# Handing out two relus and one operand split ahead of the values' product, and one weight split behind a bank's copy

## The chip, the core and the metric

One core of a Trainium2 chip runs the kernel. Its engines work from queues of their own, each in order: TensorE (PE in the profile; PEld are its weight loads), VectorE (DVE), ScalarE (ACT), GpSimd (POOL) and SyncE (SP), which issues most transfers. An instruction waits for the results of other engines at the head of its queue, and everything behind it in that queue waits with it. The metric is the device time of one execution in microseconds, as the median of several runs.

## What is computed

```
xn = layernorm(x)                                  # x: 2048 x 512, fp32
q, k, v = split(xn @ wqkv)                         # 32 heads of 16
phi(t) = where(t > 0, t + 1, exp(t)) + 1e-6
kv = sum_s phi(k)_s v_s^T ;  z = sum_s phi(k)_s     # for each head
att = (phi(q) kv) / (phi(q) z + 1e-6) @ wo
mlp = relu(xn @ w1 + b1)^2 @ w2 + b2                # 512 -> 1376 -> 512
out = x + att + mlp
```

## The kernel before

**Precision.** A factor of a product is split into an upper half (a copy rounded to the matmul's format, made on ScalarE) and a lower half (the rest, a subtraction on VectorE). `three` and `product` then run three matmuls for each pair: upper by upper, upper by lower, lower by upper. `split(h, l, src, eh, el)` makes both halves. So each operand costs one ScalarE and one VectorE instruction before the third matmul can run; the first two need the upper half of the weights only.

**Two parts.** The first part (to about 100 us) normalises x, transposes it, projects the keys, and sums `kx`, the keys by the tokens. The second part is the loop over n = 0 and 1, each for two blocks of 512 tokens, x1 and x2. There, chunks of wq and w1 (256 columns at a time) are multiplied with both blocks by Winograd's scheme: seven half-size products (`A11`, `A12`, `S1` to `S4`, `A22`) in place of eight. Their factors are sums of quarters of the weights (S1 to S4) and of the tokens (T1 to T4), each split in two halves. The loop over p goes over the chunks: q, w1, q, and then w1 to the end.

**Places.** For the products there are four banks, `banks`, taken as A, `before`, B and C. At p = 0, TensorE runs product A (`A11`), product B (`A12`) and product C (`S1` with T1), six matmuls each; then `matrix(0)` and `matrix(1)`, three each, into `pm0` and `pm1`; then the second product into A (`S2` with T2), `matrix(2)`, the second into C (`S4`), `matrix(3)`, and `S3` with T3. The banks of `pz` and `pz0b` are among those that `banks` takes over, C's being that of `pz`. Operand halves stand in `aop`; the raw chunks of weights and S1 to S4 share six places, "raw".

**Around the change.** The last chunk of w1 has only 96 columns and is computed by itself for both blocks: `pz` (x1) and `pz0b` (x2), with `plain_1`. Between them run the last matmuls of `kx`. `values()` (line 870) multiplies `kx` by wv into `pkv` (lines 871 to 878), masks it by heads into `kv` on VectorE (line 880), and splits that into `kvt` (upper half on ScalarE, lower on VectorE). `matrix(j)` multiplies `kvt` by wo; its results are the attention's 512 x 512 matrix.

**The order by hand.** The program is in a manual schedule: each engine runs its instructions in the order of the text. `extra` is a list of small pieces of work (splits, differences for T, operands), and `more()` takes the next few off it, by a table of counts. `do(list, k)` takes k pieces. When `values()` is called in the old text, five pieces are left: the lower half of T1's second part; the split of S1 and S2; the lower half of T2's second part; the split of `A22`; the split of S3 and S4. The call of `more()` behind `values()` takes the first two of these, and `do(extra, len(extra))` the last three, behind the two relus (line 476, a helper's; called at 953 and 954), which move `pz` and `pz0b` out of their banks into `r2c`.

**w2.** `piece_2(f, at)` loads chunk f of w2 (256 KB) and returns two pieces, the upper half on ScalarE and the lower on VectorE. For the last chunk (f = 10, 96 rows in three loads), the upper half's piece also has five casts on GpSimd, which lay out a quarter of it four times (`w2q`), and the lower half is two subtractions. `next_2(t)` (line 974) does what is left of the present chunk, and calls `piece_2` for the next, so that its load is issued. `next_2(0)`, at line 986, does the last chunk's halves and issues the load of chunk 0. Inside p, `c11` (line 1050) is product A copied out of its bank on ScalarE; VectorE adds it to B (line 1055). The first matmuls that read the last chunk of w2 are those of `last_2` at p = 1.

The order of instructions by engine around the change, in the old text:

```
ScalarE: A's operand | kvt upper | S1,S2 upper | relu pz | relu pz0b | A22 upper | S3,S4 upper | w2 upper | c11 | t5 | T3 ...
VectorE: A's operand | kv | kvt lower | T1 lower | S1,S2 lower | T2 lower | A22 lower | S3,S4 lower | w2 lower x2 | q <- B + c11 | T3 lower x2 ...
```

Of the kernel before, what the change touches and what calls it, by code (L numbers as in the profile page):

```python
# [18 lines left out]
def kernel(  # L19
# [58 lines left out]
    def bank(name, tag="ps"):  # L78
        return psum.tile([P, 512], F32, name=name, tag=tag)

    def w512(name, tag, bufs):
        return work.tile([P, 512], F32, name=name, tag=tag, bufs=bufs)
# [26 lines left out]
    def copy(eng, o, i, bias=0.0):  # L109
        if eng == "act":  # L110
            nc.scalar.activation(o, i, AF.Copy, bias=bias)  # L111
        elif bias:
            ENG[eng].tensor_scalar(o, i, bias, None, op0=OP.add)
        else:
            ENG[eng].tensor_copy(o, i)

    def split(h, l, src, eh, el):
        copy(eh, h, src)
        ENG[el].tensor_tensor(out=l, in0=src, in1=f32(h), op=OP.subtract)  # L119
# [76 lines left out]
    def piece_2(f, at):  # L196

        h, l = w2s[f] = [w2r[at // 2][:, at % 2 * 2 + u] for u in range(2)]
        if f < NF - 1:
            t = raw(f"r2_{f}", w2[f * P:(f + 1) * P, :])  # L200
            return [lambda: copy("act", h, t), lambda: rest_of(l, t, h)]


        t = w512(f"r2_{f}", "raw", 6)
        for a, o, n in units(f):
            nc.sync.dma_start(t[a:a + n], w2[o:o + n, :])

        def high():
            copy("act", h, t)
            copy("pool", l[2 * Q:], h[:2 * Q])  # L210
            if "q" not in w2s:
                w2s["q"] = work.tile([P, D], F32R, name="w2q", tag="w2q")
                for k in range(TB):
                    copy("pool", w2s["q"][k * Q:(k + 1) * Q], h[2 * Q:3 * Q])

        def low():
            rest_of(l[:2 * Q], t[:2 * Q], h[:2 * Q])
            rest_of(h[3 * Q:], t[3 * Q:], h[3 * Q:])

        return [high, low]  # L220
# [191 lines left out]
    def steps_of(t, j, done=False, parts=False):  # L412


        o = q[t][:, j]
        tiles = []
        blocks = lambda ap: ap.rearrange("p (r c) -> p r c", c=32)
        heads_of = lambda ap: ap.rearrange("p (h d) -> p h d", h=H)
        by_heads = lambda ap: ap.rearrange("p (r h) d -> p r h d", h=2)

        def weighted():
            pz = w512(f"pz{t}_{j}", "p", 6)
            tiles.append(pz)
            nc.scalar.activation(pz, o, AF.Identity, bias=zc[:, 1, j:j + 1], scale=zc[:, 0, j:j + 1])

        def sums():
            pt = w512(f"pt{t}_{j}", "p", 6)
            den = small.tile([P, H], F32, name=f"dt{t}_{j}", tag="den")
            nc.vector.transpose(blocks(pt), blocks(tiles[0]))
            nc.vector.tensor_reduce(den, heads_of(pt), axis=AX.X, op=OP.add)  # L430
            tiles.append(den)

        def quotients():
            pz, den = tiles
            nc.vector.tensor_scalar(den, den, 1e-6, None, op0=OP.add)
            nc.vector.reciprocal(den, den)
            nc.vector.transpose(by_heads(heads_of(pz)), by_heads(den[:, :, None].to_broadcast([P, H, D // H])))

        def divide():
            nc.vector.scalar_tensor_tensor(o, o, 1e-6, tiles[0], op0=OP.add, op1=OP.mult)  # L440

        def into_parts():
            a = aT[t, j] = places.pop(0)
            split(a[:, 0], a[:, 1], o, "act", "dve")

        return [lambda: phi_T(o, o)][done:] + [weighted, sums, quotients, divide] + [into_parts][:parts]
# [28 lines left out]
    def relu(o, i, f):  # L475
        nc.scalar.activation(o, i, AF.Relu, bias=b1s[:, f:f + 1])

    def plain_1(ps, w, x):

        for j in range(NJ):  # L480
            three(ps, [w[:, u, j * P:(j + 1) * P] for u in range(2)],
                  [x[u][:, j, :] for u in range(2)], j == 0, j == NJ - 1)

    def product(ps, a, b, first=False, last=False):

        for j in range(2):
            for n, (u, v) in enumerate(PASSES):
                nc.tensor.matmul(ps, lhsT=a[u][:, j * P:(j + 1) * P], rhs=b[v][:, j, :],  # L488
                                 start=first and j == 0 and n == 0, stop=last and j == 1 and n == 2,
                                 skip_group_check=True)  # L490
# [50 lines left out]
    for i0 in range(0, NT, TB):  # L541
# [5 lines left out]
        n = TB if i0 >= NPE else NPE - NDVE  # L547
# [175 lines left out]
    def do(what, k=1):  # L723
        for _ in range(k):
            if what:
                what.pop(0)()
# [39 lines left out]
    extra, counts = [], [[0, 0, 0, 0, 0, 1, 1, 0, 0, 1, 2, 2, 0, 1, 4, 1, 2]]  # L766

    def more(i=None):

        if i is None or i > 12:  # L770
            do(extra, counts[0].pop(0))
# [98 lines left out]
    def values():  # L870
        ps = bank("pkv", "acc")
        for c in range(NJ):
            for j in range(NJ):
                at = slice(j * P, (j + 1) * P)

                nc.tensor.matmul(ps[:, at], lhsT=wvs[:, c, at], rhs=kxs[c // 2][:, c % 2, at],  # L876
                                 start=c == 0 and j == 0, stop=c == NJ - 1 and j == NJ - 1,
                                 skip_group_check=True)
        t = w512("kv", "p", 6)
        nc.vector.tensor_tensor(out=t.rearrange("p (j d) -> p j d", j=NJ), in0=ps.rearrange("p (j d) -> p j d", j=NJ),  # L880
                                in1=heads[:, None, :].to_broadcast([P, NJ, P]), op=OP.mult)
        kvt[0] = work.tile([P, 2, 512], F32R, name="kvt", tag="r3")
        split(kvt[0][:, 0], kvt[0][:, 1], t, "act", "dve")
# [16 lines left out]
    for n in range(2):  # L900
# [42 lines left out]
        if n == 0:  # L943

            more()
            pz2 = bank("pz0b")
            plain_1(pz2, z, x2)
            more()
            values()
            more()  # L950

            rz = r2[1]
            relu(rz, pz, NF - 1)
            relu(r2[NF - 1], pz2, NF - 1)
            do(extra, len(extra))
            w2next = piece_2(NF - 1, 0)
        else:
            w2next = []
            pz = bank(f"pz{n}", "acc")
            plain_1(pz, z, x1)  # L960
# [13 lines left out]
        def next_2(t):  # L974

            do(w2next, 2 - highs.pop(0))
            if t + 1 < NF and (n == 0 or t >= TB - 1):
                f = w2order[t + 1]
                w2next.extend(piece_2(f, place(f)))

        def high_2():
            do(w2next)
            highs[0] = 1

        highs = [0] * NF
        next_2(0)


        banks = [bank(f"b{n}_{k}") for k in range(4)]
# [29 lines left out]
        def step(k=1):  # L1019

            for _ in range(k):
                do(steps[t1] or steps[t2])

        for p in range(NO + 1):
# [24 lines left out]
            if kind:  # L1049
                c11 = w512(f"c11_{n}_{p}", "p", 6)  # L1050
                copy("act", c11, A)
                product(B, A12, [x[:, 2:] for x in x1], True, True)
                if kind == "w":
                    high_2()
                nc.vector.tensor_tensor(out=c11 if kind == "w" else q[t1][:, fa], in0=B, in1=c11, op=OP.add)
                if kind == "w":
                    relu(c11, c11, fa)
                else:
                    steps[t1] += steps_of(t1, fa, parts=True)
                step(at_p[0])  # L1060
# [261 lines left out]
```

## Time and profile before

| | us |
|---|---|
| median of 3 runs | 415.05 (414.95 to 415.22) |
| the profiled execution | 415.3 |
| its span in the trace | 413.6 |
| TensorE busy, of the span | 408.6 |
| mean granted clock of TensorE | 0.998 |

A row of the timeline reads: start, length, engine, line and operation, output and inputs by the program's names, shape, count, and in brackets the idle time of the engine just before it with the instruction that ended it. Rows with a count are several instructions of one kind in a row, merged. The chain of waits is followed back from the last instruction to what released it, and its pieces are listed in order of time. Matmuls are pipelined and their ends are modelled, so a wait shows in the weight loads (PEld) more plainly than in the matmuls. A row of the windows reads: the stretch, its length, then for TensorE, weight loads, VectorE, ScalarE and GpSimd the busy time and in brackets the count, then the granted clock, the share of the transfer engines and their rate in GB/s.

### The profile page before, as it was taken

How to read it: one execution, taken by the hardware profiler on the slowest of the kernel's cores; microseconds unless marked ns; L12 is line 12 of the kernel's file. 1: busy time of each engine (PE TensorE's matmuls, PEld its weight loads, DVE VectorE, ACT ScalarE, POOL GpSimd, SP SyncE). 2: the span in 40 equal slices, each digit the busy share in tenths (PEclk: the TensorE clock that was granted, in tenths of full speed). 3: DMA queues.
4: the chain of work that ended last, by engine and by line, in shares of the span. 5: the costliest groups of instructions: out<-in, count | busy, mean ns of one | idle time of the engine just before them, and what ended most of it. 6: DMA issues, size and time to landing. Idle time of an engine off the chain costs nothing.

```text
span 413.6 us, 5427 instructions
## 1 busy us (share of the span) xinstructions
PE 408.6 (99%) x1835; PEld 336.9 (81%) x1835; DVE 314.5 (76%) x584; ACT 270.2 (65%) x487; POOL 50.0 (12%) x70
## 2 busy tenths in 40 slices
PE   8999999999999999999999999999999999999996
PEld 7788888888888888888878888888888888878885
DVE  6895667797699898998439996468989685449843
ACT  5867767756668888789547731567588857737420
POOL 3241222230130000020000040100000200000310
PEclk9999999999999999999999999999999999999999
DMA  7789572710321312264267991411120871025602
GB/s 248 272 247 353 204 228 101 234 48 2 102 77 52 101 41 72 93 177 78 89 246 251 385 198 75 129 52 48 54 79 25 228 183 47 2 86 168 103 0 101
DMA packets 44925, 54.62 MB, mean 132 GB/s; under 512 B 7905, under 2 KB 29153, under 8 KB 43618
## 3 DMA queue, kind: packets, MB, share of 16 engines
q1 hardware_dynamic: 42594, 50.09, 37.1%
q0 software_dynamic: 2304, 4.20, 6.5%
q8 instruction: 14, 0.23, 0.2%
q14 instruction: 13, 0.11, 0.1%
HBM read 41.16 MB, written 13.11 MB: 131 GB/s over the span
## 4 chain that ended last, share of the span: by engine, by line
PE 97%; DMA 1%; ACT 0%; SPq 0%; DVE 0%; issue 0%
PE acc L130 37%; PE b L488 32%; PE kx L389 11%; PE pk L370 11%; PE acc L499 2%; PE pz L130 1%; DMA rk<-in_A_wqkv_dram 1%; PE pkv L876 1%; PE pm L130 1%; PE pz0b L130 1%; PE b L130 1%; PE pt L309 1%; PE acc L506 0%; SPq L159 0%; PE end L130 0%; ACT wkh L111 0%
## 5 line engine op out<-in xcount | busy, mean ns | idle before, releaser
L130 PE MATMUL acc<-w2r,s 128*128 128x512 f32 x477 | 112.9, 390 | 0.0
L130 PEld LDWEIGHTS acc<-w2r,s 128*128 128x128 f32 x477 | 89.4, 188 | 19.3 <-issue 0.7
L488 PE MATMUL b<-T,aop 128*128 128x512 f32 x336 | 83.9, 390 | 0.0
L488 PEld LDWEIGHTS b<-T,aop 128*128 128x128 f32 x336 | 62.8, 188 | 13.9 <-DVE aop L119 0.4
L389 PE MATMUL kx<-pk,tok 128*128 128x512 f32 x192 | 46.8, 392 | 0.0
L389 PEld LDWEIGHTS kx<-pk,tok 128*128 128x128 f32 x192 | 35.6, 188 | 8.0 <-DVE pk L378 0.6
L488 PE MATMUL b<-xs0h,aop 128*128 128x512 f32 x112 | 36.9, 390 | 0.0
L1005 POOL DMA_DIRECT2D res<-in_B_b_dram x16 | 14.1, 1099 | 182.4 <-DVE dt L430 64.1
L130 PE MATMUL acc<-mh,aTsr 128*128 128x512 f32 x112 | 35.6, 389 | 0.0
L119 POOL TENSOR_TENSOR tok<-xp,tok 128x512 fp32r<-128x512 f32 x16 | 22.3, 1393 | 55.1 <-ACT tok L111 55.1
L1013 DVE TENSOR_TENSOR res<-acc,res 128x512 f32<-128x512 f32 x16 | 11.0, 692 | 23.1 <-PE acc L130 18.5
L122 DVE TENSOR_TENSOR w2r<-r,w2r 128x512 fp32r<-128x512 f32 (+2 forms) x35 | 25.2, 721 | 0.1
L111 ACT ACTIVATE aop<-S 128x512 fp32r<-128x512 f32 x28 | 17.5, 624 | 11.1 <-DVE S L705 11.1
L130 PEld LDWEIGHTS acc<-mh,aTsr 128*128 128x128 f32 x112 | 21.0, 188 | 4.4
L488 PEld LDWEIGHTS b<-xs0h,aop 128*128 128x128 f32 x112 | 21.0, 188 | 4.3
L119 DVE TENSOR_TENSOR aop<-S,aop 128x512 fp32r<-128x512 f32 x28 | 19.5, 697 | 4.3 <-ACT aop L111 3.9
L119 DVE TENSOR_TENSOR s<-c,s 128x512 fp32r<-128x512 f32 x20 | 13.6, 689 | 11.0 <-ACT s L111 11.0
L130 PE MATMUL acc<-ml,aTsr 128*128 128x512 f32 x56 | 21.8, 389 | 0.0
L488 PE MATMUL b<-xs0l,aop 128*128 128x512 f32 x56 | 21.8, 389 | 0.0
L111 ACT ACTIVATE w2r<-r 128x512 fp32r<-128x512 f32 x32 | 19.6, 619 | 2.6 <-DMA out_dram<-res 2.0
L111 ACT ACTIVATE T<-Tf 128x512 fp32r<-128x512 f32 x16 | 9.5, 628 | 16.5 <-DVE Tf L648 16.4
L488 PE MATMUL b<-xs1h,aop 128*128 128x512 f32 x56 | 19.5, 389 | 0.0
(197 smaller groups left out, 770.0 us busy)
## 6 DMA issues: line engine op xcount, KB each, us to landing
r<-in_B_w_dram SPq DMA_DIRECT2D x49, 256.0 KB, 3.0
res<-in_A_x_dram SPq DMA_DIRECT2D x8, 512.0 KB, 4.7
res<-in_B_b_dram POOLq DMA_DIRECT2D x16, 256.0 KB, 5.7
out_dram<-res SPq DMA_DIRECT2D x15, 256.0 KB, 2.1
x<-in_A_x_dram SPq DMA_DIRECT2D x5, 512.0 KB, 5.8
via<-xp SPq DMA_DIRECT2D x5, 512.0 KB, 2.7
xg<-via SPq DMA_DIRECT2D x20, 128.0 KB, 2.9
xTd<-t SPq DMA_DIRECT2D x8, 256.0 KB, 3.4
```

What stands on the lines that cost most here:

```text
L111: nc.scalar.activation(o, i, AF.Copy, bias=bias)
L119: ENG[el].tensor_tensor(out=l, in0=src, in1=f32(h), op=OP.subtract)
L122: nc.vector.tensor_tensor(out=l, in0=src, in1=f32(h), op=OP.subtract)
L130: nc.tensor.matmul(ps, lhsT=a[u], rhs=b[v], start=first and n == 0, stop=last and n == 2)
L309: nc.tensor.transpose(t[k][:, at:at + P], xp[i][:, j * P:(j + 1) * P], ident)
L370: nc.tensor.matmul(ps, lhsT=cols(i)[u][:, j, slot(i)], rhs=w[v][:, j, :], start=first and n == 0, stop=last and n == len(steps) - 1)
L389: nc.tensor.matmul(kxp[c], lhsT=tok[i][:, u, c * P:(c + 1) * P], rhs=pk[i][:, v], start=i == 0 and (u, v) == first, stop=i == NT - 1 and ( ...
L488: nc.tensor.matmul(ps, lhsT=a[u][:, j * P:(j + 1) * P], rhs=b[v][:, j, :], start=first and j == 0 and n == 0, stop=last and j == 1 and n == 2,
L499: nc.tensor.matmul(ps, lhsT=s[u][:, k * P:(k + 1) * P], rhs=w2s[NF - 1][u][:, a:z], start=first and u == 0, stop=stop and u == 1)
L876: nc.tensor.matmul(ps[:, at], lhsT=wvs[:, c, at], rhs=kxs[c // 2][:, c % 2, at], start=c == 0 and j == 0, stop=c == NJ - 1 and j == NJ - 1 ...
L1005: nc.gpsimd.dma_start(r[:, i], b2[None, :].partition_broadcast(P), accum_op=OP.add)
L1013: nc.vector.tensor_tensor(out=r[:, a:z], in0=ps, in1=r[:, a:z], op=OP.add)
```

## The change

The relus of `pz` and `pz0b`, and the first two pieces of `extra` (T1's lower half, the split of S1 and S2), are handed out before `values()` instead of behind it. The call of `more()` behind `values()` goes, so that `do(extra, len(extra))` takes the last three pieces as before. For n = 0, `next_2(0)` is called at p = 0 behind the copy of A's bank into `c11` instead of ahead of the products; for n = 1 it stays where it was.

```diff
             plain_1(pz2, z, x2)
             more()
-            values()
-            more()
 
             rz = r2[1]
             relu(rz, pz, NF - 1)
             relu(r2[NF - 1], pz2, NF - 1)
+            do(extra, 2)
+            values()
             do(extra, len(extra))
             w2next = piece_2(NF - 1, 0)
...
         highs = [0] * NF
-        next_2(0)
+        if n:
+            next_2(0)
...
                 c11 = w512(f"c11_{n}_{p}", "p", 6)
                 copy("act", c11, A)
+                if n == 0 and p == 0:
+                    next_2(0)
                 product(B, A12, [x[:, 2:] for x in x1], True, True)
```

## The prediction

> **What bounds the kernel now.** I read the page's first part, then the chain of waits, then the stretch that the edit touches engine by engine.
>
> ```profile
> span 413.6 us, 5427 instructions
> PE 408.6 (99%) x1835; PEld 336.9 (81%) x1835; DVE 314.5 (76%) x584; ACT 270.2 (65%) x487; POOL 50.0 (12%) x70
> PE 97%; DMA 1%; ACT 0%; SPq 0%; DVE 0%; issue 0%
> ```
>
> TensorE sets the time. The chain that ended last is 97% matmuls, so an edit on the other engines counts only where TensorE waits for what it moves. The chain in order of time (start, length, what, how many matmuls) shows where that is:
>
> ```profile
> 102.98 3.57 PE pkv L876 x32
> 106.56 4.58 PE b L488 x18
> 111.14 1.39 PE pm L130 x6
> 112.53 1.37 PE b L488 x6
> ...
> 123.45 1.81 PE acc L499 x8
> ...
> 260.12 4.08 PE b L488 x18
> ...
> 410.29 0.02 issue
> ```
>
> The first 18 matmuls of the Winograd stage, products A, B and C of p = 0 (six each), took 4.58 us. The same 18 in the second pass, at 260.12, took 4.08 us. So 0.50 us was lost once. From 106.56 to 410.29 every piece of the chain is TensorE's, so a loss here is carried to the end whole. The page's busy share hides it; the weight loads show it (the first of A, the last of B, then C's, then pm0's):
>
> ```profile
> 106.28 0.19 PEld L488 LDWEIGHTS b<-xs0h,aop 128*128 128x128 f32 x1
> ...
> 108.71 0.19 PEld L488 LDWEIGHTS b<-xs0h,aop 128*128 128x128 f32 x1
> 109.24 0.30 PEld L488 LDWEIGHTS b<-T,aop 128*128 128x128 f32 x2 [0.34 <-ACT r2c L476]
> 109.93 0.76 PEld L488 LDWEIGHTS b<-T,aop 128*128 128x128 f32 x4 [0.40 <-DVE aop L119]
> 110.74 1.35 PEld L130 LDWEIGHTS pm<-wo,kvt 128*128 128x128 f32 x6
> ```
>
> C's first load stood 0.34 us, until the relu of pz had let its bank go; the third, 0.40 us, until S1's lower half was there. ScalarE and VectorE at that place:
>
> ```profile
> 102.71 0.61 ACT L111 ACTIVATE aop<-rq 128x512 fp32r<-128x512 f32 x1
> 107.32 0.63 ACT L111 ACTIVATE kvt<-kv 128x512 fp32r<-128x512 f32 x1 [4.00 <-DVE kv L880]
> 107.86 0.61 ACT L111 ACTIVATE aop<-S 128x512 fp32r<-128x512 f32 x1
> 108.50 0.69 ACT L476 ACTIVATE r2c<-pz,b1s 128x512 f32<-128x512 f32 x1
> 109.08 0.68 ACT L476 ACTIVATE r2c<-pz0b,b1s 128x512 f32<-128x512 f32 x1
> 109.65 0.42 ACT L111 ACTIVATE aop<-rq 128x256 fp32r<-128x256 f32 x1
> 109.96 0.63 ACT L111 ACTIVATE aop<-S 128x512 fp32r<-128x512 f32 x1
> 110.48 0.63 ACT L111 ACTIVATE w2r<-r 128x512 fp32r<-128x512 f32 x1
> 111.00 0.60 ACT L111 ACTIVATE c<-b 128x512 f32<-128x512 f32 x1
> ```
>
> ```profile
> 103.35 0.69 DVE L119 TENSOR_TENSOR aop<-rq,aop 128x512 fp32r<-128x512 f32 x1 [1.65 <-ACT aop L111]
> 106.59 0.69 DVE L880 TENSOR_TENSOR kv<-pkv,heads 128x512 f32<-128x512 f32 x1 [2.55 <-PE pkv L876]
> 107.98 0.69 DVE L119 TENSOR_TENSOR kvt<-kv,kvt 128x512 fp32r<-128x512 f32 x1 [0.70 <-ACT kvt L111]
> 108.59 0.68 DVE L122 TENSOR_TENSOR T<-Tf,T 128x512 fp32r<-128x512 f32 x1
> 109.19 0.69 DVE L119 TENSOR_TENSOR aop<-S,aop 128x512 fp32r<-128x512 f32 x1
> ```
>
> ScalarE sat idle 4.00 us ahead of kvt and VectorE 2.55 us ahead of kv, both for the values' product, with the relus and S1's split queued behind.
>
> **The change part by part.** No instruction is added or removed; two groups change place in their queues.
>
> The relus, T1's last rest and the split of S1 and S2 go in front of the values. ScalarE is done with A's operand at 103.32. The relus and S1's upper half start 0.58, 0.57 and 0.64 us apart by the rows above (108.50, 109.08, 109.65; 107.86 to 108.50), so they run from about 103.3 to 105.1, inside the idle 4.00 us. VectorE does T1's rest from 104.04 to 104.7 and S1's lower half from 105.1 to 105.8, inside its idle 2.55 us. Both engines are free 0.8 us before the values end, so kv still starts at 106.59 and kvt is whole at 108.67. If that cover were gone, each 0.1 us past 106.59 would delay kvt by 0.1 us.
>
> C is due after A and B, a third of 4.08 each: at 106.56 + 2 x 1.36 = 109.28. By then its bank has been free for five microseconds and S1 whole for three and a half. Both waits end, C ends at 106.56 + 4.08 = 110.64, and pm0 follows with kvt two microseconds old. What is late next is nothing that I find: T2's last rest moves to 108.6 to 109.3 and is due at about 112.
>
> The price has two ends. Gross, the two waits are 0.34 + 0.40 = 0.74 us, but a weight load runs ahead of its matmul and part of a wait is lead that nobody missed. Net, from A's first load to pm0's, it is 110.74 - 106.28 = 4.46 us against 4.08, 0.38 us. I take the chain's 0.50, since it measures the same 18 matmuls twice.
>
> TensorE's own row could be read otherwise:
>
> ```profile
> 106.56:111.14 4.58, 4.58 (x19) 3.23 (x19) 3.85 (x7) 3.79 (x8) 0.00 (x0) 1.00 0.60 156
> ```
>
> Matmuls are busy 4.58 of 4.58 us there (the first number after the length), loads 3.23 (the second). By the first alone the sum would be zero. The Trainium skill (Perfetto Trace Analysis, Identifying the Most-Contended Engine) says that matmul occupancy is no measure of the distance to roofline and points to the share of the weight loads; the trace agrees, since the loads are busy 71% here against 81% over the whole span, while matmul occupancy shows no gap.
>
> The w2 edit. ScalarE copies c11 first and then w2's upper half. A's product ends at about 107.9, so c11, third in the queue behind the a22 and S3 splits, runs at about 108.7 to 109.3 instead of 111.00, and w2's half at about 109.3 to 109.9 instead of 110.48. Nothing of TensorE's is behind either: A's bank is wanted for the next product at about 112.0 (112.53 in the chain), and w2's chunk for the first last_2 (the piece at 123.45). On VectorE w2's two rests stay in front of q<-b. The same call loads w2's chunk 0 into the place that S1 leaves, and starts GpSimd's five casts:
>
> ```profile
> 106.43 0.97 SPq L184 DMA_DIRECT2D r<-in_B_w_dram  x2
> 109.91 0.35 SPq L165 DMA_DIRECT2D r<-in_B_w_dram  x1
> r<-in_B_w_dram SPq DMA_DIRECT2D x49, 256.0 KB, 3.0
> 112.55 3.64 POOL L115 CAST w2q<-w2r 32x512 fp32r<-32x512 f32 x4
> 113.67 2.04 DVE L122 TENSOR_TENSOR T<-Tf,T 128x512 fp32r<-128x512 f32 x2
> 119.66 1.28 DVE L122 TENSOR_TENSOR T<-Tf,T 128x512 fp32r<-128x512 f32 x2
> 113.95 0.67 ACT L111 ACTIVATE aop<-r 128x512 fp32r<-128x512 f32 x1
> 116.48 1.53 PE L488 MATMUL b<-T,aop 128*128 128x512 f32 x6
> ```
>
> SP has no other issue between the two places of the call, so the load keeps its rank behind the two w1 chunks of line 184, and can only start earlier (S1 is free at 105.8, not 109.88). At the window's 156 GB/s all three loads, 768 KB, take about 5 us from 106.4, to 111.4; ScalarE wants the first w1 chunk at 113.4. Cost nothing; if that cover is gone, splits of the next block wait, and these have over a microsecond until TensorE needs them.
>
> The casts come about 1 us earlier. Beside them two of T3's rests took 2.04 us, without them two of T4's 1.28: each lost 0.38 us. T3 is due at 116.48 - 0.50 = 115.98, and its last rest at the fifth of six matmuls, 116.89. Its rests start once ScalarE has copied t5 and T3 behind C, about 112.5, and end at about 114.5, so the slack is over 2 us, since VectorE has shed 1.2 us of work from this stretch. The price at TensorE is between 0 and nothing measurable; I take 0. The Trainium skill (SBUF — State Buffer, Who interferes with whom) says that a VectorE instruction with two SBUF inputs and a GpSimd instruction that reads SBUF block each other fully. The 0.38 us, well under one cast (0.87 us), bears out contention but not a full block. By the rule, five casts would add 5 x (0.87 - 0.38) = 2.45 us, T3 would end at about 116.95 and the gain would shrink by 0.1 us at most.
>
> The sum: the profiled execution took 415.3 us, 1.7 us around its span of 413.6; less 0.50 it is a span of 413.1 and 414.8 us. That execution lies 0.25 us over the median 415.05, so the median should become **414.55 us**, which is 0.12% less.
>
> **The rivals.** *The loss only moves.* C is freed, but something else holds TensorE by the same half microsecond before pm2: kvt, T2's rest or the freed bank of A. For it: kvt's split feeds the very next matmuls. Against it: the slacks of 2 to 3 us above. Time: 415.05 us.
>
> *The front is not ready, and the values pay.* Nothing in this trace shows a relu waiting, so it shows only that the relus could run by 108.50, not when they first could. If something held them until then (their place, or a count that TensorE passes on late), kv and kvt would stand behind them: relus 108.50 to 109.65, S1's upper half to 110.3, its lower half to 110.95, kv to 111.6, kvt's halves to 112.2 and 112.9. pm's third matmul would start at 112.9 and its last end four steps of 0.227 later, at 113.8, against 112.53: 1.3 us lost, 416.3 us. It decides from the front ending 0.8 us late for kv, 3.2 us late (0.8, and kvt's lower half has 111.1 - 108.67 = 2.4) for TensorE, and 3.7 us late for a time above today's. Against it: the banks were filled by 102.98, S1 was summed long before, and the relus' place was last read early:
>
> ```profile
> 87.86 0.42 DVE L705 TENSOR_TENSOR S<-rq,S 128x256 f32<-128x256 f32 x1
> L294 DVE STREAM_TRANSPOSE t<-xg x2: 703/704/705, 35.5 to 41.3; 128x512 f32<-128x512 f32 x2
> ```
>
> *More than the chain shows.* The gross 0.74 us comes back: 414.3 us.
>
> **How the numbers follow.** The forecast 0.76, the loss that moves 0.11, the values pay 0.05, the gross gain 0.07, and 0.01 for a loss that I do not see. A measurement of this kernel can tell about 0.2%, 0.83 us, from no change. The forecast, the gross gain and the loss that moves all lie inside that. Faster by more takes a time under 414.22: the gross gain with a run 0.1 us lower, or the forecast with one 0.3 lower; 0.09. Slower by more takes a time over 415.88, which the paying values and the unseen loss give; 0.06. The rest is 0.85. The range goes from 414.2 (gross gain, and 0.1 us for the lowest of the runs shown, 414.95 against 415.05) to 415.2 (no gain, at the highest run, 415.22).
>
> **What would show it.** In the profile after: no wait of a weight load for r2c or for S1's split; the first 18 matmuls of the stage at 4.08 us; both relus between 103 and 105 and S1's lower half ahead of kv; kv still at about 106.6; c11 before w2's upper half, both before 110; pm0 at about 110.6 and every later piece of the chain 0.5 us earlier. It is wrong if kv starts later than 106.8, if a new wait stands ahead of pm or A's second product, or if the half microsecond is gone at 112 and back at 124.

## The result, and the profile after

| | before | after |
|---|---|---|
| median, us (22 runs each) | 415.13 (414.94 to 415.71) | 414.50 (414.35 to 414.76) |
| ratio | | 0.9983, 95% interval 0.9978 to 0.9989 |
| span of the profiled execution, us | 413.6 | 412.7 |

The changed kernel is 0.63 us faster by the medians (0.15%) and 0.17% by the ratio, which is worked out from the single runs: less than the 0.2% that was called no change, and yet the interval stays clear of 1 with this many runs. The chain of waits after, in the pieces that answer to those shown of before:

```profile
102.79 3.57 PE pkv L876 x32
106.36 4.13 PE b L488 x18
110.50 1.37 PE pm L130 x6
111.87 1.37 PE b L488 x6
...
124.61 9.52 PE b L488 x42
134.12 2.72 PE acc L130 x12
```

The first 18 matmuls take 4.13 us in place of 4.58. Everything was already 0.19 us earlier at pkv (102.79 against 102.98), which comes from the start of this execution and not from the change (it is there at 92 already, 91.91 against 92.10 in the two chains). A second piece is shorter too, which the prediction had not listed. It stands at 125 in the chain of before:

```profile
125.26 9.64 PE b L488 x42
134.90 2.74 PE acc L130 x12
```

Its 42 matmuls took 9.64 us, now 9.52. So the first 18 gave 0.45 us, pm 0.02 and these 0.12; from pkv to the matmuls behind that piece the whole stretch shrank from 134.90 - 102.98 = 31.92 to 134.12 - 102.79 = 31.33, by 0.59 of the 0.63 us; the trace of one execution and the medians need not agree closer than that. The weight loads of before show what held TensorE there:

```profile
131.68 1.32 PEld L488 LDWEIGHTS b<-T,aop 128*128 128x128 f32 x6
133.25 1.23 PEld L488 LDWEIGHTS b<-T,aop 128*128 128x128 f32 x6 [0.25 <-DVE t L1037]
```

TensorE waited 0.25 us until VectorE had added t and so let a bank go. VectorE was late because it had been working almost without a pause since 108 (a row of the windows of before; VectorE's busy time is the fourth figure, behind length, PE and PEld):

```profile
108.00:133.00 25.00, 25.00 (x109) 20.14 (x108) 24.68 (x45) 20.52 (x39) 5.50 (x6) 1.00 0.29 83
```

The changed kernel has 24.59 us there, hardly less, since VectorE fills what it gains with the work behind. So the busy time does not tell the two apart; what counts is when VectorE gets to t.

Of the changed kernel, the last weight load of B, those of C and those of pm0 and pm1, without a wait in any:

```profile
108.52 0.19 PEld L488 LDWEIGHTS b<-xs0h,aop 128*128 128x128 f32 x1
108.75 1.32 PEld L488 LDWEIGHTS b<-T,aop 128*128 128x128 f32 x6
110.11 1.33 PEld L130 LDWEIGHTS pm<-wo,kvt 128*128 128x128 f32 x6
```

ScalarE, and then VectorE, of the changed kernel:

```profile
103.15 0.69 ACT L476 ACTIVATE r2c<-pz,b1s 128x512 f32<-128x512 f32 x1
103.74 0.68 ACT L476 ACTIVATE r2c<-pz0b,b1s 128x512 f32<-128x512 f32 x1
104.31 0.63 ACT L111 ACTIVATE aop<-S 128x512 fp32r<-128x512 f32 x1
107.13 0.63 ACT L111 ACTIVATE kvt<-kv 128x512 fp32r<-128x512 f32 x1 [2.19 <-DVE kv L880]
...
108.49 0.58 ACT L111 ACTIVATE c<-b 128x512 f32<-128x512 f32 x1
108.97 0.62 ACT L111 ACTIVATE w2r<-r 128x512 fp32r<-128x512 f32 x1
```

```profile
104.97 0.69 DVE L119 TENSOR_TENSOR aop<-S,aop 128x512 fp32r<-128x512 f32 x1 [0.52 <-ACT aop L111]
106.40 0.69 DVE L880 TENSOR_TENSOR kv<-pkv,heads 128x512 f32<-128x512 f32 x1 [0.74 <-PE pkv L876]
107.79 0.69 DVE L119 TENSOR_TENSOR kvt<-kv,kvt 128x512 fp32r<-128x512 f32 x1 [0.70 <-ACT kvt L111]
...
112.28 2.04 DVE L122 TENSOR_TENSOR T<-Tf,T 128x512 fp32r<-128x512 f32 x2
...
131.27 0.68 DVE L1038 TENSOR_TENSOR t<-b,t 128x512 f32<-128x512 f32 x1
```

Both relus and S1's upper half stand in what was idle time, kv starts as soon as pkv is there, and t is added at 131.27 instead of 132.52: less the 0.19 us of the start VectorE is 1.06 us earlier there, and TensorE 0.59.

### The profile page after: what moved, and what is told of

It is laid out like the page before. It is cut to its first block, busy times and chain, and to the rows that moved or that the text cites. A ratio compares the mean times of both kernels' runs of the same rounds, so it can differ in the third digit from the quotient of the medians.

```text
span 412.7 us, 5426 instructions
## 1 busy us (share of the span) xinstructions
PE 407.3 (99%) x1835; PEld 336.7 (82%) x1835; DVE 314.5 (76%) x584; ACT 270.6 (66%) x487; POOL 49.6 (12%) x70
## 4 chain that ended last, share of the span: by engine, by line
PE 98%; DVE 1%; DMA 1%; ACT 0%; issue 0%
PE acc L130 37%; PE b L488 32%; PE kx L389 11%; PE pk L370 11%; PE acc L499 2%; PE pz L130 1%; PE pkv L876 1%; PE pm L130 1%; PE pz0b L130 1%; PE b L130 1%; PE pt L309 1%; DMA x<-in_A_x_dram 1%; PE acc L506 0%; DVE st L230 0%; PE end L130 0%; DVE xp L269 0%
```

## The experiments

Two theories stood at the start for the two waits of C: A, they stand one behind the other and the later one sets the loss; B, each has a share of its own. For the second gain, theory V: VectorE has no idle time from 108 to 133, so TensorE keeps what it gains at 109 only if VectorE, too, gets earlier by as much. Theory T: only C's waits counted, and VectorE has slack.

In the table, "stretch" is the time from the start of pkv to the start of the acc matmuls behind the 42, as worked out above, against that of the kernel before. It is read from the one profiled execution of each run (with six more on ScalarE the chain leaves TensorE at that place, and the end of the matmuls ahead of pkv stands for the start). Times are medians, each against the kernel before on the same chip. The ratio is worked out from the single runs and not from the two medians, so it can differ from their quotient; where the kernel before took 415.33, single runs of it reached 417.38. The expectations give absolute times and start from 415.05; on these chips the kernel before took 0.20 to 0.28 us more, so what they forecast is compared as a difference.

| run | stretch, us | time, us | before, us | ratio, 95% interval |
|---|---|---|---|---|
| relus only | +0.08 | 415.30 | 415.25 | 0.9998 (0.9989 to 1.0007) |
| split only | -0.56 | 414.62 | 415.25 | 0.9982 (0.9974 to 0.9991) |
| front only | -0.59 | 414.64 | 415.25 | 0.9984 (0.9974 to 0.9993) |
| w2 only | +0.30 | 415.57 | 415.25 | 1.0005 (0.9996 to 1.0013) |
| one more on VectorE | -0.40 | 414.65 | 415.33 | 0.9974 (0.9961 to 0.9988) |
| two more on VectorE | +0.23 | 415.40 | 415.33 | 0.9993 (0.9981 to 1.0004) |
| six more on ScalarE | +0.43 | 415.65 | 415.33 | 0.9999 (0.9987 to 1.0011) |
| T2 ahead too | -0.59 | 414.70 | 415.33 | 0.9977 (0.9965 to 0.9990) |
| T1 only ahead | -0.09 | 415.29 | 415.30 | 1.0002 (0.9993 to 1.0010) |

### The parts of the change, each alone

Relus only, against the kernel before:

```diff
-            values()
-            more()
             rz = r2[1]
             relu(rz, pz, NF - 1)
             relu(r2[NF - 1], pz2, NF - 1)
+            values()
+            more()
             do(extra, len(extra))
```

> The two relus go in front of the values, the split of S1 and S2 and the w2 split stay where they were. Theory A (the two waits of C stand one behind the other and the later one, for S1's lower half, sets the loss): the first load of C waits no more, the third still waits until S1's lower half ends at about 109.9, so the first 18 matmuls of the stage take 4.5 to 4.6 us and the time is 415.05 to 415.15. Theory B (each wait costs its own share, 0.34 and 0.40 of 0.74 us): 18 matmuls in about 4.35 us and 0.2 us faster, 414.9.

The weight loads of this run, from C's third on (the run began 1.8 us later than the others):

```profile
111.69 0.76 PEld L488 LDWEIGHTS b<-T,aop 128*128 128x128 f32 x4 [0.58 <-DVE aop L119]
```

The wait for the bank is gone, and the wait for S1's lower half is 0.58 us instead of 0.40. The stretch is no shorter: S1's lower half ended as long after the start of pkv as before (6.9 us), and C's third load waited for that. Theory A holds for the relus: the later wait took over what the first one gave up.

Split only, against the kernel before:

```diff
+            do(extra, 2)
             values()
-            more()
             rz = r2[1]
```

> T1's lower half and the split of S1 and S2 go in front of the values, the relus and the w2 split stay behind. Theory A: with S1's upper half out of ScalarE's way the relu of pz follows kvt's upper half at once and ends at about 108.6, before C is due at 108.9 to 109.3, so both waits go: 18 matmuls in 4.1 us, the wait of 0.25 us at 133 goes as well, since VectorE's two subtractions have moved into its idle time, and the time is that of the changed kernel, 414.4 to 414.6. Theory B: the relu's wait of 0.34 us remains, 18 matmuls in 4.3 us, 414.8.

Nearly the whole gain (0.56 of 0.59 us of the stretch), with the relus still behind the values. The chain and ScalarE of this run:

```profile
106.60 4.13 PE b L488 x18
```

```profile
107.36 0.63 ACT L111 ACTIVATE kvt<-kv 128x512 fp32r<-128x512 f32 x1 [3.48 <-DVE kv L880]
108.01 0.69 ACT L476 ACTIVATE r2c<-pz,b1s 128x512 f32<-128x512 f32 x1
```

The relu of pz now follows kvt directly and ends at 108.70, before C's first load (about 109.0 here). So the relu had been late only because S1's upper half stood ahead of it. Theory B is out: with the split moved there is next to nothing left for the relus' move to bring.

Front only leaves out the w2 edit; w2 only is that edit alone (both as in the change's diff).

> Relus and split in front of the values as in the changed kernel, the w2 split where it was. If the w2 edit costs and brings nothing: 414.4 to 414.6, 18 matmuls in 4.13 us, no wait at 133. If the earlier copy of c11 is what ends the wait of 0.25 us at 133: that wait stays, pieces of 42 matmuls at 9.64 us, 414.6 to 414.7.

> The w2 split behind c11 alone; relus and split of S1 and S2 behind the values as before. If the w2 edit costs and brings nothing: 415.05 to 415.15, the waits of 0.34 and 0.40 us and that of 0.25 at 133 all stay. If it ends the wait at 133: 0.12 us less, 415.0. If it costs something that the other edits hide: more than 415.3.

With the front moved, the w2 edit is worth nothing: the stretch is the changed kernel's to the hundredth. Alone, it made the stretch of its profiled execution 0.30 us longer; the times don't show that, since their interval still holds no change. VectorE and the weight loads of w2 only:

```profile
111.63 1.71 DVE L122 TENSOR_TENSOR w2r<-r,w2r 64x512 fp32r<-64x512 f32 x2 [0.21 <-ACT w2r L111]
```

```profile
121.95 1.23 PEld L488 LDWEIGHTS b<-T,aop 128*128 128x128 f32 x6 [0.20 <-ACT sz L111]
133.54 1.22 PEld L488 LDWEIGHTS b<-T,aop 128*128 128x128 f32 x6 [0.39 <-DVE t L1038]
```

With c11 ahead of it, w2's upper half came 0.48 us later (110.96 against 110.48), VectorE idled 0.21 us for it and began w2's lower half 0.29 us later than before (111.63 against 111.34). TensorE then waited 0.20 us at 122, where it had not, and 0.39 us instead of 0.25 at 133. (At 122 the row names ScalarE's sz; VectorE's sum into q, by line 1038, ended later still, at 121.83.) This was the first sign that a few tenths of a microsecond on VectorE are paid for.

### What VectorE has to spare

The changed kernel with one more subtraction on VectorE, the result not used; in the other run the range is 2:

```diff
             values()
+            for _ in range(1):
+                t2h = f32(T[2][:, 0, 0])
+                nc.vector.tensor_tensor(out=r2[0], in0=t2h, in1=t2h, op=OP.subtract)
             do(extra, len(extra))
```

> The changed kernel with one more VectorE subtraction of 128 x 512 (0.6 us, its result is not used) behind kvt's lower half. Theory V (VectorE has no idle time from 108 to about 133, so what it sheds before 106 decides whether TensorE can keep its gain at 133): the first 18 matmuls stay at 4.13 us, VectorE stands about 0.6 us later at 132 against TensorE 0.65 us earlier than in the kernel before, so the wait for t at 133 is back at about 0.2 to 0.3 us and the time is 414.55 to 414.75. Theory T (only the two waits of C counted, VectorE has 2 us of slack): no wait, 414.4 to 414.6.

> The same with two such subtractions, 1.2 us, as much as the change moved off VectorE's busy stretch. Theory V: the first 18 matmuls stay at 4.13 us, but the wait at 133 grows to about 0.8 us and gives the gain back, 415.0 to 415.3, the time of the kernel before. Theory T: 414.4 to 414.6.

The weight loads with one more, and with two more:

```profile
132.73 1.23 PEld L488 LDWEIGHTS b<-T,aop 128*128 128x128 f32 x6 [0.31 <-DVE t L1041]
```

```profile
120.02 1.22 PEld L488 LDWEIGHTS b<-T,aop 128*128 128x128 f32 x6 [0.22 <-ACT T L111]
121.82 1.22 PEld L488 LDWEIGHTS b<-T,aop 128*128 128x128 f32 x6 [0.58 <-ACT sz L111]
133.42 1.24 PEld L488 LDWEIGHTS b<-T,aop 128*128 128x128 f32 x6 [0.38 <-DVE t L1041]
```

Two of these rows name ScalarE. ScalarE of the run with two more, and then its chain of waits:

```profile
117.79 0.63 ACT L111 ACTIVATE aop<-S 128x512 fp32r<-128x512 f32 x1 [3.12 <-DVE S L705]
```

```profile
121.10 0.61 DVE q L1041
121.71 0.14 issue
121.85 1.63 PE b L488 x6
```

ScalarE made T4's upper halves, which the load at 120.02 wanted, only after it had stood 3.12 us for VectorE's sums S (1.70 us in the changed kernel). And the chain puts the wait at 121.82 down to VectorE's sum into q, which ended after sz did. From kvt's lower half at 107.94 to this matmul at 121.85 it holds instructions of VectorE alone. So all three waits go back to VectorE.

Theory V. With 0.6 us more the wait at 133 is back at 0.31 us; the stretch says 0.19 us lost, which the time, with its wide interval, neither shows nor excludes. With 1.2 us more the gain is gone, while the two waits of C are still absent. Counted from the start of pkv, VectorE added t after 29.75 us there and after 28.48 in the changed kernel: 1.27 us later, about the two subtractions and no more. The gain went at three places, not at 133 alone as was expected, the largest at 121.8.

Six more copies on ScalarE, in front of the values:

```diff
             do(extra, 2)
+            for _ in range(6):
+                copy("act", r2[0], f32(T[2][:, 0, 0]))
             values()
```

> The changed kernel with six more ScalarE copies of 128 x 512 in front of the values (results not used), so that kvt's upper half starts about 1.2 us later, at 108.3. Theory T (as the prediction has it, TensorE's own need for kvt decides, with 2.4 us to spare): 414.4 to 414.6. Theory V: VectorE idles 1.2 us ahead of kvt's lower half, stands 1.2 us later in its busy stretch, and the wait at 133 takes the gain: 415.0 to 415.3.

ScalarE, VectorE and the weight loads of this run:

```profile
104.95 3.94 ACT L111 ACTIVATE r2c<-T 128x512 f32<-128x512 f32 x6
108.80 0.61 ACT L111 ACTIVATE kvt<-kv 128x512 fp32r<-128x512 f32 x1
```

```profile
109.45 0.69 DVE L119 TENSOR_TENSOR kvt<-kv,kvt 128x512 fp32r<-128x512 f32 x1 [2.22 <-ACT kvt L111]
```

```profile
108.87 1.32 PEld L488 LDWEIGHTS b<-T,aop 128*128 128x128 f32 x6
110.23 1.33 PEld L130 LDWEIGHTS pm<-wo,kvt 128*128 128x128 f32 x6
```

Counted from pkv, kvt's upper half is 1.5 us later than in the changed kernel, and TensorE does not wait for kvt at pm, just as theory T has it. But VectorE idled 2.22 us, and waits at 120, 122 and 133 (0.33, 0.59 and 0.47 us), as in the run before this one, took the gain. From kvt's lower half at 109.45 to TensorE's wait at 122 the chain of this run holds instructions of VectorE alone. Theory T is out.

T2's lower half ahead as well, ahead of S1's:

```diff
-            do(extra, 2)
+            t2_low = extra.pop(2)
+            do(extra, 1)
+            t2_low()
+            do(extra, 1)
             values()
```

> The changed kernel with T2's lower half ahead of the values as well, in the 0.52 us that VectorE waits there for S1's upper half. Both theories: no wait of TensorE is left for it to end, so 414.4 to 414.6; VectorE stands 0.6 us earlier at 108 to 133. If it is faster by more than 0.1 us, VectorE still costs TensorE something that no wait shows.

VectorE of this run:

```profile
109.88 1.71 DVE L122 TENSOR_TENSOR w2r<-r,w2r 64x512 fp32r<-64x512 f32 x2 [0.21 <-ACT w2r L111]
...
128.37 0.69 DVE L410 SCALAR_TENSOR_TENSOR q<-q,phi 128x512 f32<-128x512 f32 x1 [0.21 <-ACT phi L409]
```

No wait was left and none went: the stretch is the changed kernel's. The expectation that VectorE would stand 0.6 us earlier up to 133 failed. It idled, among others, for ScalarE's upper half of w2 and for its phi, and t was added 28.48 us after the start of pkv, as in the changed kernel. So what VectorE saved was lost in waits for others, and what more room on VectorE would bring TensorE is not shown.

T1's lower half alone ahead, against the kernel before:

```diff
+            do(extra, 1)
             values()
-            more()
+            do(extra, 1)
             rz = r2[1]
```

> The kernel before with only T1's lower half ahead of the values; relus, the split of S1 and S2 and the w2 split stay. S1's lower half then ends at about 109.3 instead of 109.9, and the relu of pz still at 109.2. Theory A and V together: the first load of C waits 0.34 us as before, the third no more, so the first 18 matmuls take 4.25 to 4.35 us; VectorE stands 0.6 us earlier and TensorE 0.3 us, so the wait at 133 goes as well; 0.4 us less than before, 414.7 to 414.9. Rival: as in the run with the relus alone, one wait that stays takes all, 415.1 to 415.3.

The chain, and then the weight loads and VectorE of this run:

```profile
106.53 4.35 PE b L488 x18
...
125.03 9.76 PE b L488 x42
```

```profile
109.22 1.23 PEld L488 LDWEIGHTS b<-T,aop 128*128 128x128 f32 x6 [0.34 <-ACT r2c L476]
133.14 1.23 PEld L488 LDWEIGHTS b<-T,aop 128*128 128x128 f32 x6 [0.37 <-DVE t L1038]
```

```profile
110.08 0.43 DVE L119 TENSOR_TENSOR aop<-rq,aop 128x256 fp32r<-128x256 f32 x1 [0.23 <-ACT aop L111]
...
111.21 1.70 DVE L122 TENSOR_TENSOR w2r<-r,w2r 64x512 fp32r<-64x512 f32 x2
```

The first 18 matmuls came out as expected (4.35 us, the bank's wait alone), but half of that gain was given back at 133, where the 42 matmuls took 9.76 us instead of 9.64. The expectation that VectorE would stand 0.6 us earlier failed: it ran into ScalarE's queue, which was unchanged, idled 0.23 us for the upper half of A22, and reached w2 at 111.21 instead of 111.34. So the time VectorE saves has to be fed by ScalarE, and that takes S1's upper half out of its queue as well. The rival named the right time by luck: it had one wait take all, while here half of the gain went and the rest (0.09 us of the stretch) is too small for the times to show.

## Why the prediction was right, and where it was not

**The bound and the place.** Right: TensorE's chain, and the loss at C. Not right: "0.50 us was lost once" and "carried to the end whole". The chain held a second loss at 133, and in the run with T1 alone half of what C gained was lost again there.

**The price.** The forecast of 0.50 us came near 0.63 in part by luck, since one term was too large and another was left out. At C, 0.45 came back of the 0.50: 18 matmuls took 4.13 us and not 4.08 as in the second pass. The 0.05 us that stayed are no wait of C, whose six matmuls run 1.53 us from their first start to the end of the 18 (108.97 to 110.50) and 1.52 in the second pass (262.68 to 264.20); they lie in A and B, behind pkv, and no run says why. And 0.12 us at 133 was missing from the sum. The failed step is "What is late next is nothing that I find": the wait for t stood in the trace of before, 24 us away from the edit. The change removed it because it shed VectorE work, a fact that the prediction had in hand (1.2 us) and used only as cover.

**The relus and the split.** The prediction gave each its own wait. The runs show one cause: the split of S1, in the wrong place, held up C by its own lateness (behind T1's lower half on VectorE) and, through ScalarE's queue, by the relu's. Moving these two pieces alone is worth nearly all of it (0.56 of 0.59 us).

**The w2 edit at nothing.** Right where it stands, wrong as a statement on the edit: "Nothing of TensorE's is behind either" does not hold for the kernel before. There w2's upper half held up VectorE, VectorE held up TensorE, and the edit alone lengthened the stretch by 0.30 us.

**The cover.** "The slack is over 2 us" was true of T3, the nearest consumer (its lower halves ended at 114.32, or 114.51 with the start added back, as forecast, and no load waited), and not of VectorE. The room for more work on VectorE was under 0.6 us, by the wait that one more subtraction brought back. For the same reason the rival of the paying values has the wrong threshold: it was to decide for TensorE from 3.2 us of lateness of the front, which is 2.4 us of kvt, and 1.5 us of kvt were enough to lose the whole gain, with no wait at pm.

**The casts.** The prediction read the 0.38 us that VectorE lost beside a cast, against 0.87 us for a cast, as no full block. That reading is wrong: the 0.87 us hold the cast's own wait for VectorE. The last section shows the rows. So the 2.45 us "by the rule" count again what the trace of before already held.

**The schedule.** S1's lower half ended at 105.66 (105.8 forecast), kvt at 108.48 (108.67), pm0 began at 110.50 (110.64): with the 0.19 us of the start added back, all within 0.05 us. The rival of the loss that only moves did not occur in the changed kernel. In the run with T1 alone it occurred by half, at 133 and not ahead of pm2, where that rival looked.

## What to carry to other kernels

In this kernel, what TensorE gained by a wait removed was kept only where VectorE, the next-busiest engine, got earlier too. So before pricing an edit, list every wait of the busiest engine, the far ones as well, and see which are fed by an engine without idle time. Of two waits in a row on one engine, ending the first alone gained nothing here, and ending the second alone gained half of what both cost at that place; look for a cause that makes both late. Move work from a full stretch into idle time together with what feeds it: half of the pair brought next to nothing.

## What was not expected of the hardware

With two more subtractions, other VectorE instructions fell beside GpSimd's casts than in the changed kernel. The same two splits, of A22 and of S3 and S4, in the changed kernel and then in that run, with the casts of that run:

```profile
109.00 0.42 DVE L119 TENSOR_TENSOR aop<-rq,aop 128x256 fp32r<-128x256 f32 x1
109.34 0.69 DVE L119 TENSOR_TENSOR aop<-S,aop 128x512 fp32r<-128x512 f32 x1
```

```profile
110.48 0.83 DVE L119 TENSOR_TENSOR aop<-rq,aop 128x256 fp32r<-128x256 f32 x1
111.24 1.09 DVE L119 TENSOR_TENSOR aop<-S,aop 128x512 fp32r<-128x512 f32 x1
```

```profile
110.24 0.80 POOL L115 CAST w2r<-w2r 64x512 fp32r<-64x512 f32 x1 [18.37 <-ACT w2r L111]
111.10 0.69 POOL L115 CAST w2q<-w2r 32x512 fp32r<-32x512 f32 x1
```

Each lost 0.40 us, the short one as much as the long one. The reason can be read from the ends. The first cast ended at 111.04 and the short subtraction (256 columns) at 111.31, 0.27 us later; the next cast at 111.79 and the long one (512 columns) at 112.33, 0.54 us later. Counted from the end of the cast, twice the columns took twice the time. The changed kernel has the same one step on: its casts at 112.15, 112.81 and 113.83 ended at 112.75, 113.77 and 114.79, and the three VectorE instructions beside them (T3's two lower halves and the split behind) at 113.30, 114.31 and 115.33, 0.54 to 0.55 us after each. The first of these casts began beside an addition that reads a bank, and took 0.60 us; the two that began beside a subtraction took 0.96. So the casts waited as well.

The Trainium skill (SBUF — State Buffer, Summary: rules for kernel authors) says that the second to issue blocks fully until the first is done, for a VectorE instruction with two SBUF inputs beside a GpSimd instruction that reads SBUF. The trace agrees: the two take turns. What a VectorE instruction loses is what is left of the cast when it starts, less about 0.15 us by the ends above, and not a fixed delay: it was 0.46 us in the run with one more (sz at 120.88, 1.15 us against 0.69) and 0.30 us in the kernel before (the split at 122.28, 0.99 us against 0.69).
